# A fused DeltaNet and SwiGLU kernel: the small products ordered by tile shape and mixed across units, and 32x32 blocks moved through DRAM

## The chip, the cores and the metric

The kernel runs on one core of one Trainium2 chip. The metric is device time in microseconds (us): the median of the runs. The core has a matrix engine (PE, or TensorE; its weight loads are a queue of their own, PEld), a vector engine (DVE), a scalar engine (ACT), a general engine (POOL) and a queue that issues DMAs (SP). Each engine works through its instructions in the order of the program, and waits where an operand isn't there.

## What is computed

Two parts, both in float32. The first is a delta-rule attention over 4 batches (B), 8 heads (H), 768 tokens (S), head width 48 (D). With the keys normed to length 1, each head runs over its tokens:

```python
y[:, :, t] = np.einsum('bhd,bhde->bhe', q[:, :, t], state)
v_old = np.einsum('bhde,bhd->bhe', state, kt)
state = state + bt[:, :, :, None] * np.einsum('bhd,bhe->bhde', kt, vt - v_old)
```

The second takes y as 3072 rows of 384 and computes a gated feed-forward net (FFN): RMS norm with gain, g = xn @ w_gate, val = xn @ w_val, out = (silu(g) * val) @ w_out, with d_ff = 1536. The weights arrive as 64-bit floats, and the kernel turns their bits into float32 itself.

## The kernel before, in words

The tokens are cut into 6 chunks (NCH) of 128. A unit is one batch in one chunk, with its 8 heads; there are 24 units (n = 4c + b). In a chunk the recurrence becomes a triangular system, which is solved by halves of 64 (lo and hi) and quarters of 32. Each unit goes through four generators, and a chunk through a fifth:

- `prepare` norms the keys, transposes q and k on PE (p_t) into `kqt`, and makes all products of keys with keys and with queries (p_g, L293: four matrices of 64x64 inputs, 192 columns each). One DVE instruction per p_g (L300) multiplies by a mask and writes `gp`.
- `invert`, once a chunk for all 32 heads, inverts the 32x32 unit triangles on DVE: four 32x32 block transposes bring `gp` into `gblk` (L316), 31 steps of two instructions (L325, L334) build the inverse `ttb`, and transposes and copies (L336 to L351) put it into `tt`.
- `merge` joins the 32-quarters into 64-halves: p_v (L366) takes 32 rows and 64 columns of the array, p_w (L379) 32 by 32, and p_x (L388) 64 by 64 for the coupling of the halves, with copies on ACT between them.
- `recur` subtracts what the state already knows (p_k, L413), solves for u (p_z: L425 for both halves by 64x64, then L433 for the lower half, which needs the upper half's u), updates the state (p_s, L443), and makes the output p_y from the state (L453) and from u (L463 for the upper half, 64 rows by 64 columns; L466 for the lower half, 128 rows by 64 columns; the two alternate head by head). Then come the RMS norm and a transpose into `xt`.
- `ffn`, two a chunk, takes 256 tokens: for each of 12 slices of d_ff six matrix products into p_gv (L532), silu on ACT, a product h_f on DVE (L543), and two products into p_o (L519).

A float32 product is two PE instructions, so the trace counts twice as many as the program.

The order of the work is made by a plan. Each generator has a start time and yields after each piece with a step in plan units, and `run_plan` always continues the generator with the smallest time. One FFN piece (six instructions of p_gv, or four of p_o) is one unit; a chunk has 72. So small pieces fall between FFN pieces on PE. In a chunk, all merges stand at 46 to 48, and the recurs start at 50.1 and every 2.7 later. `weights` converts the 36 weight tiles on DVE and ACT, from plan time -69 on, one every 2.1 units. All small products share four PSUM buffers (tag "delta"). SP issues all DMAs, in order.

Of the kernel before, what the change touches and what calls it, by code (L numbers as in the profile page):

```python
# [10 lines left out]
FP32 = mybir.dt.float32  # L11
# [7 lines left out]
C = 128  # L19
HC = 64  # L20
DP = 64
W = 32
K1, K0, Q0, Q1 = 0, 2, 3, 4
# [4 lines left out]
def kernel(  # L28
# [11 lines left out]
):  # L40

# [23 lines left out]
    work = ctx.enter_context(tc.tile_pool(name="work", bufs=2))  # L65
    psum = ctx.enter_context(
# [8 lines left out]
    mask = const.tile([128, 3 * HC], FP32, name="mask")  # L75
# [16 lines left out]
    kqt = [const.tile([128, NP, 5, HC], FP32, name=f"kqt{b}") for b in range(B)]  # L92
    gp_all = const.tile([128, BH, 3 * HC], FP32, name="gp")
# [3 lines left out]
    back = const.tile([128, W, BH], FP32, name="back")  # L97

    vraw = {}

# [79 lines left out]
    raws = []  # L180
# [8 lines left out]
    def weights(dt):  # L189
        with tc.tile_pool(name="bits", bufs=2) as bits:  # L190
            fetch(bits)
            fetch(bits)
            yield dt
            for i, (dst, src) in enumerate(todo):
# [13 lines left out]
                )  # L208
                nc.scalar.activation(
# [16 lines left out]
                nc.vector.scalar_tensor_tensor(  # L226
                    out=exp,
                    in0=high,
                    scalar=0x80000000,
                    in1=exp,  # L230
                    op0=ALU.bitwise_and,
                    op1=ALU.bitwise_or,
                )
                nc.vector.scalar_tensor_tensor(
                    out=dst, in0=low, scalar=2.0**-52, in1=dst, op0=ALU.mult, op1=ALU.add
                )
                nc.vector.tensor_tensor(out=dst, in0=dst, in1=exp_f, op=ALU.mult)
                yield dt


    def prepare(n):
# [29 lines left out]
        nc.scalar.copy(kqt[b][:, :, Q0 : Q1 + 1], p_t)  # L271
# [10 lines left out]
        nc.scalar.copy(kqt[b][:, :, K0], p_t[:, :, 0])  # L282
        nc.scalar.copy(kqt[b][:, :, K1], p_t[:, :, 1])
        yield 2

        for g in range(NP // 2):
            p_gs = [ps_delta([128, 2, 3 * HC], "p_g") for par in range(2)]
            for jj in range(2):
                pair = kqt[b][:, 2 * g + jj]
                for par, i in ((0, 0), (1, 1), (0, 1), (1, 0)):  # L290
                    lo = slice(DP * par, DP * (par + 1))
                    rhs = pair[lo, K1 : K1 + 5 : 2] if i else pair[lo, K0 : K0 + 3]
                    nc.tensor.matmul(  # L293
                        p_gs[par][HC * i : HC * (i + 1), jj].rearrange("p (a t) -> p a t", a=3),
                        pair[lo, K1 if i else K0],
                        rhs,
                        skip_group_check=True,
                    )
            for par in range(2):
# [6 lines left out]
            yield 1  # L306

# [3 lines left out]
    def invert(c, dt):  # L311
        nc.gpsimd.memset(ttb, 0.0)
        nc.gpsimd.memset(ttb.rearrange("p j i -> p (j i)")[:, 0 : W * W : W + 1], 1.0)
        for a in range(NBLK):
            p, o = slice(W * a, W * (a + 1)), W * (a % 2)
            nc.vector.transpose(  # L316
                out=gblk[p], in_=gp_all[p, :, o : o + W].rearrange("p x j -> p j x")
            )
        yield dt
        for i in range(W - 1):  # L320
            n = W - 1 - i
            shape = [128, n, i + 1]
# [10 lines left out]
            to = ttb[:, i + 1 :, 0 : i + 1]  # L333
            nc.vector.tensor_tensor(out=to, in0=to, in1=tmp, op=ALU.add)  # L334
            yield dt
        nc.vector.transpose(out=back, in_=ttb)  # L336

        def place(a, copy):
            p, o = slice(W * a, W * (a + 1)), W * (a % 2)
            copy(tt_all[p, :, o : o + W].rearrange("p x j -> p j x"), back[p])  # L340

        place(1, nc.scalar.copy)
        place(3, nc.scalar.copy)

        nc.vector.tensor_tensor(
            out=gblk,
            in0=ttb.rearrange("p m s -> p s m"),
            in1=nbeta[:, c, None, :].to_broadcast([128, W, W]),
            op=ALU.mult,
        )  # L350
        nc.vector.transpose(out=ttb, in_=gblk)  # L351
        yield dt
        place(0, nc.vector.tensor_copy)
        place(2, nc.vector.tensor_copy)
# [266 lines left out]
```

## Time and profile before

| what | value |
|---|---|
| median of 3 runs | 1129.95 us (1114.73 to 1134.86) |
| the profiled execution | 1130.28 us, span 1128.5 us |
| PE busy | 1006.1 us (89% of the span) |
| DVE busy | 485.6 us (43%) |
| ACT busy | 275.8 us (24%) |
| chain that ended last | PE 70%, DVE 21%, ACT 4% |

In a row of a timeline stand the start (us from the span's start), the length (us), the engine, the line, the operation, the tile written and those read, the array tile used (rows*columns), the shape, and xcount, the number of instructions that are merged into the row. What is in brackets is the engine's idle time before it and what ended it. The lengths of PE rows overlap a little, since products are pipelined; start to start is the better reading.

### The profile page before, as it was taken

Reading aid. Unit: us, or ns where it says so; the run is one execution under the profiler, and the core shown is the slowest. Engines: PE = TensorE matmul, PEld = TensorE weight load, DVE = VectorE, ACT = ScalarE, POOL = GpSimd, SP = SyncE. Lnnn points to the kernel's source line nnn. Section 1 sums busy time; section 2 is a strip of 40 time slices with the busy share of each in tenths; the row PEclk is TensorE's granted clock in tenths of the full one; section 3 lists DMA queues with packets and bytes.
Section 4 is the critical chain, followed back from the end, with each engine's and each line's share of the span. In section 5 each row is a group of like instructions: output and inputs, shape, how many; then the busy total and the mean of one; then the engine's idle time right before and its main releaser. Section 6 shows DMA issues by size and latency. Waiting matters only on the chain.

```text
span 1128.5 us, 18814 instructions
## 1 busy us (share of the span) xinstructions
PE 1006.1 (89%) x8142; PEld 773.5 (69%) x8142; DVE 485.6 (43%) x1116; ACT 275.8 (24%) x590; POOL 83.3 (7%) x97
## 2 busy tenths in 40 slices
PE   5202997989999989999989999989999989999998
PEld 3102975767877767777767877767777767777776
DVE  5998347483222394222395122295132394211110
ACT  3766446113112112112112212112212113111011
POOL 6000003000021000022000022000021000000000
PEclk9555559998979996998998989998999998978999
DMA  6533222000111000011100011100011000000000
GB/s 146 138 95 96 72 72 76 8 15 2 29 22 35 15 15 1 18 34 29 22 15 1 16 36 29 22 15 1 16 37 28 1 15 1 2 1 15 1 15 15
DMA packets 84882, 34.43 MB, mean 31 GB/s; under 512 B 77088, under 2 KB 80160, under 8 KB 84800
## 3 DMA queue, kind: packets, MB, share of 16 engines
q1 hardware_dynamic: 84800, 33.24, 11.8%
q8 instruction: 64, 1.05, 0.4%
q14 instruction: 18, 0.15, 0.0%
HBM read 28.51 MB, written 4.72 MB: 29 GB/s over the span
## 4 chain that ended last, share of the span: by engine, by line
PE 70%; DVE 21%; ACT 4%; issue 1%; POOL 1%; POOLq 0%; ACTq 0%
PE p_gv L532 27%; PE p_o L519 12%; DVE tmp L325 6%; DVE ttb L334 5%; PE p_y L466 5%; PE p_y L463 5%; DVE gblk L316 4%; PE p_v L366 4%; PE p_g L293 3%; PE p_x L388 2%; PE p_z L425 2%; PE p_z L433 2%; PE p_w L379 2%; ACT tt L340 2%; PE p_k L413 1%; DVE h_f L543 1%
## 5 line engine op out<-in xcount | busy, mean ns | idle before, releaser
L519 PE MATMUL p_o<-wo_sb,h_f 128*128 128x384 f32 x576 | 220.3, 507 | 23.1 <-DVE h_f L543 23.1
L532 PE MATMUL p_gv<-xt,wv_sb 128*128 128x256 f32 x864 | 232.0, 408 | 0.0
L532 PE MATMUL p_gv<-xt,wg_sb 128*128 128x256 f32 x864 | 231.4, 406 | 0.0
L532 PEld LDWEIGHTS p_gv<-xt,wg_sb 128*128 128x128 f32 x864 | 169.2, 201 | 44.4 <-issue 2.6
L532 PEld LDWEIGHTS p_gv<-xt,wv_sb 128*128 128x128 f32 x864 | 171.6, 205 | 28.0 <-issue 3.1
L543 DVE TENSOR_TENSOR h_f<-sil,p_gv 128x256 f32<-128x256 f32 x144 | 59.9, 416 | 254.9 <-ACT sil L541 254.4
L519 PEld LDWEIGHTS p_o<-wo_sb,h_f 128*128 128x128 f32 x576 | 108.7, 196 | 78.5 <-DVE h_f L543 29.4
L541 ACT ACTIVATE sil<-p_gv 128x256 f32<-128x256 f32 x144 | 55.2, 384 | 413.0 <-PE p_gv L532 395.0
L366 PE MATMUL p_v<-tt,gp 32*64 32x32 f32 x768 | 44.6, 285 | 74.7 <-ACT tt L340 74.7
L366 PEld LDWEIGHTS p_v<-tt,gp 32*64 32x64 f32 x768 | 43.1, 207 | 79.6 <-ACT tt L340 79.6
L325 DVE SCALAR_TENSOR_TENSOR tmp<-gblk,nbeta,ttb 128x31 f32<-128x31 f32 (+15 forms) x186 | 74.3, 399 | 4.6
L300 DVE TENSOR_TENSOR gp<-p_g,mask 128x384 f32<-128x384 f32 x96 | 49.2, 551 | 52.5 <-PE p_g L293 52.5
L466 PE MATMUL p_y<-u,gp 128*64 128x48 f32 x384 | 66.3, 259 | 0.0
L334 DVE TENSOR_TENSOR ttb<-ttb,tmp 128x31 f32<-128x31 f32 (+15 forms) x186 | 63.5, 341 | 5.0
L463 PE MATMUL p_y<-u,gp 64*64 64x48 f32 x384 | 65.2, 254 | 0.0
L293 PE MATMUL p_g<-kqt 64*64 64x192 f32 x768 | 51.6, 365 | 12.8 <-DVE gp L300 6.5
L485 ACT ACTIVATE sq<-p_y 128x384 f32<-128x384 f32 x24 | 11.8, 491 | 185.7 <-PE p_y L466 185.7
L293 PEld LDWEIGHTS p_g<-kqt 64*64 64x64 f32 x768 | 28.9, 144 | 35.0 <-issue 13.9
L466 PEld LDWEIGHTS p_y<-u,gp 128*64 128x64 f32 x384 | 40.8, 150 | 11.9
L463 PEld LDWEIGHTS p_y<-u,gp 64*64 64x64 f32 x384 | 40.0, 146 | 13.0
L316 DVE STREAM_TRANSPOSE gblk<-gp 32x1024 f32<-32x1024 f32 x24 | 46.2, 1926 | 0.5
L252 POOL TENSOR_TENSOR knrm<-ksum,half 128x8 f32<-128x8 f32 x24 | 39.4, 1645 | 58.4 <-DVE ksum L250 58.3
(88 smaller groups left out, 893.2 us busy)
## 6 DMA issues: line engine op xcount, KB each, us to landing
kpad<-in_k_dram SPq DMA_DIRECT2D x24, 192.0 KB, 2.7
qpad<-in_q_dram SPq DMA_DIRECT2D x24, 192.0 KB, 2.6
v_raw<-in_v_dram SPq DMA_DIRECT2D x24, 192.0 KB, 3.1
raw<-in_moe_w_gate_dram SPq DMA_DIRECT2D x12, 384.0 KB, 3.2
raw<-in_moe_w_val_dram SPq DMA_DIRECT2D x12, 384.0 KB, 3.2
raw<-in_moe_w_out_dram SPq DMA_DIRECT2D x12, 384.0 KB, 3.0
out_dram<-o_sb SPq DMA_DIRECT2D x24, 192.0 KB, 1.9
beta_sb<-in_beta_dram SPq DMA_DIRECT2D x1, 96.0 KB, 3.3
```

The lines of the kernel that those rows point to most:

```text
L293: nc.tensor.matmul(p_gs[par][HC * i : HC * (i + 1), jj].rearrange("p (a t) -> p a t", a=3), pair[lo, K1 if i else K0], rhs, skip_group_che ...
L300: nc.vector.tensor_tensor(out=gp[b][:, 4 * g + par : 4 * g + 4 : 2], in0=p_gs[par], in1=mask[:, None, :].to_broadcast([128, 2, 3 * HC]), o ...
L316: nc.vector.transpose(out=gblk[p], in_=gp_all[p, :, o : o + W].rearrange("p x j -> p j x"))
L325: nc.vector.scalar_tensor_tensor(out=tmp, in0=gblk[:, i, i + 1 :, None].to_broadcast(shape), scalar=nbeta[:, c, i : i + 1], in1=ttb[:, i : ...
L334: nc.vector.tensor_tensor(out=to, in0=to, in1=tmp, op=ALU.add)
L366: nc.tensor.matmul(p_v[HC * (a // 2) : HC * (a // 2 + 1), h], gp[b][w, h, 0:HC], tt[b][w, h, W:HC], skip_group_check=True,)
L463: nc.tensor.matmul(p_y[lo, h], sc[lo, h, HC : 2 * HC], u[lo, h], start=first, stop=True, skip_group_check=True)
L466: nc.tensor.matmul(p_y[hi, h], sc[:, h, 2 * HC : 3 * HC], u[:, h], start=first, stop=True, skip_group_check=True)
L519: nc.tensor.matmul(p_o[i], h_f[:, i * C : (i + 1) * C], wo_sb[:, f], start=(f == 0), stop=(f == FT - 1),)
L532: nc.tensor.matmul(p_gv[:, i], w_sb[:, t, f * 128 : (f + 1) * 128], xt[:, t], start=(t == 0), stop=(t == KT - 1),)
L541: nc.scalar.activation(out=sil, in_=p_gv[:, 0], func=ACTF.Silu)
L543: nc.vector.tensor_tensor(out=h_f, in0=sil, in1=p_gv[:, 1], op=ALU.mult)
```

## The change

The change has five parts.

1. P U. `gp` gets four blocks a head instead of three, with a block of zeros below the upper half's scores, so that both halves of p_y from u use all 128 rows (128x64 tiles, L435).
2. Order. `merge` and `recur` of four units become one generator a chunk, `recur(c, dt)`. It goes through the units s = -3 to 5 in three pieces each: `inner` (64x64 tiles: p_z of unit s, its lower half for unit s-1, p_x of unit s+1), `outer` (128x64 tiles: p_k of unit s+1, p_y and p_s of unit s-1), `corner` (32x32 tiles: p_v of unit s+3 and p_w of unit s+2). In each piece the products of the units alternate head by head.
3. Blocks. The diagonal 32x32 blocks go from `gp` to DRAM (`gd`) and from there into `gblk`; the inverse goes to DRAM (`td`, and `nd` for its scaled form) and from there into `tt` and `ne`. The DVE transposes and the copies are gone.
4. Eviction of p_g. Instead of one DVE instruction there are two ACT copies and three smaller DVE instructions, and the mask is 64 wide.
5. Plan. All FFN pieces stand 16 units later against the rest; weights follow a list of steps, and the last three DVE instructions of a weight tile are issued one tile later.

```diff
-K1, K0, Q0, Q1 = 0, 2, 3, 4
+Q0, K0, Q1, K1 = range(4)
...
+            nc.gpsimd.memset(gp_all[HC:C, :, 0:HC], 0.0)
...
             for par in range(2):
+                to = gp[b][:, 4 * g + par : 4 * g + 4 : 2].rearrange("p h (a t) -> p h a t", a=4)
+                p_g = p_gs[par]
+                nc.scalar.copy(to[:, :, K0], p_g[:, :, K0])
+                nc.scalar.copy(to[hi, :, K1], p_g[hi, :, K1])
                 nc.vector.tensor_tensor(
-                    out=gp[b][:, 4 * g + par : 4 * g + 4 : 2],
-                    in0=p_gs[par],
-                    in1=mask[:, None, :].to_broadcast([128, 2, 3 * HC]),
-                    op=ALU.mult,
+                    out=to[lo, :, Q0], in0=p_g[lo, :, Q0], in1=over[lo], op=ALU.mult
+                )
+                nc.vector.tensor_copy(out=to[lo, :, Q1], in_=p_g[lo, :, Q1])
+                nc.vector.tensor_tensor(
+                    out=to[hi, :, Q1], in0=p_g[hi, :, Q1], in1=over[hi], op=ALU.mult
                 )
             yield 1
+        if b == 0:
+            gds[c] = dram.tile([128, W, W], FP32, name="gd")
+        for a in range(NBLK):
+            o = diagonal(a)
+            nc.sync.dma_start(
+                out=gds[c][a * BH + b * H : a * BH + (b + 1) * H].rearrange("h r j -> r h j"),
+                in_=gp[b][W * a : W * (a + 1), :, o : o + W],
+            )
+        if b == B - 1:
+            nc.sync.dma_start(out=gblk, in_=gds.pop(c))
...
-        for a in range(NBLK):
-            p, o = slice(W * a, W * (a + 1)), W * (a % 2)
-            nc.vector.transpose(
-                out=gblk[p], in_=gp_all[p, :, o : o + W].rearrange("p x j -> p j x")
-            )
...
+        nc.sync.dma_start(out=td, in_=ttb)
...
+        nc.sync.dma_start(out=nd, in_=gblk)
+        for b in range(B):
+            for a in (1, 3, 0, 2):
+                o = W * (a % 2)
+                nc.sync.dma_start(
+                    out=tt[b][W * a : W * (a + 1), :, o : o + W],
+                    in_=td[a * BH + b * H : a * BH + (b + 1) * H].rearrange("h r j -> r h j"),
+                )
+            for a in (0, 2):
+                nc.sync.dma_start(
+                    out=ne[W * a : W * (a + 1), b * H : (b + 1) * H],
+                    in_=nd[a * BH + b * H : a * BH + (b + 1) * H].rearrange("h r j -> r h j"),
+                )
...
+            for h in range(H):
+                for p, place in ((lo, Q0), (hi, Q1)):
+                    nc.tensor.matmul(
+                        p_y[p, h],
+                        gp[b_y][:, h, HC * place : HC * (place + 1)],
+                        u[:, h],
...
+        for s in range(-3, B + 2):
+            inner(s, s - 1, s + 1)
+            yield dt
+            outer(s + 1, s - 1)
+            yield dt
+            corner(s + 3, s + 2)
+            if s - 2 in units:
+                transpose_y(B * c + s - 2, ys.pop(s - 2))
+            yield dt
...
-    at(-69, weights(2.1))
     for c in range(NCH):
-        t0 = CYC * (c - 1)
+        t0 = CYC * c
         for b in range(B):
-            n = B * c + b
-            at(t0 - 1 + 5 * b, prepare(n))
-            at(t0 + 46 + 0.6 * b, merge(n, 2.7))
-            at(t0 + 50.1 + 2.7 * b, recur(n, 3))
-        at(t0 + 25.3, invert(c, 0.55))
+            at(t0 - 60 + 5 * b, prepare(B * c + b))
+        at(t0 - 32.7, invert(c, 0.55))
+        at(t0 - 9, recur(c, 1.2))
         for g in range(B // 2):
-            at(CYC * c + CYC // 2 * g, ffn(B // 2 * c + g))
+            at(t0 + 16 + CYC // 2 * g, ffn(B // 2 * c + g))
+
+    at(-59, weights([2.4] * 10 + [0.7] * 3 + [16] + [1.0] * 3 + [2.0] * 19))
```

The first place is PE at the output of a unit in the second chunk, before. A row names the line, the operation, the tile written, the tiles read and the shape written.

```order
L532 MATMUL p_gv<-xt,wg_sb 128x256 x3
L443 MATMUL p_s<-u,kpad_82 64x48 x8
L453 MATMUL p_y<-state_85,kqt_90 64x96 x8
L463 MATMUL p_y<-u,gp 64x48
L466 MATMUL p_y<-u,gp 64x48
```

The last two rows come eight times in turn, once a head, before the next FFN piece. With the change the same place on PE reads:

```order
L587 MATMUL p_gv<-xt,wg_sb 128x256 x3
L470 MATMUL p_k<-state_89,kqt_94 64x96 x8
L470 MATMUL p_y<-state_87,kqt_92 64x96 x8
L435 MATMUL p_y<-u,gp 64x48 x16
L448 MATMUL p_s<-u,kpad_84 64x48 x8
```

All of it uses 128x64 tiles now, the sixteen products from u stand in one row, and the p_k of a unit two further on has moved in front of them.

The second place is PE a little earlier in the same chunk, where units are merged and solved. Before, it reads:

```order
L413 MATMUL p_k<-state_87,kqt_92 64x96 x8
L425 MATMUL p_z<-v_raw,tt 64x48 x16
L532 MATMUL p_gv<-xt,wg_sb 128x256 x3
L433 MATMUL p_z<-u,x_2131 64x48 x8
L532 MATMUL p_gv<-xt,wv_sb 128x256 x3
```

With the change PE has there the end of a corner, an FFN piece and the begin of an inner:

```order
L401 MATMUL p_v<-tt,gp 32x32
L408 MATMUL p_w<-vs,ne 32x32
L574 MATMUL p_o<-wo_sb,h_f 128x384 x2
L488 MATMUL p_z<-v_raw,tt 64x48 x2
L497 MATMUL p_z<-u,x_2239 64x48
L506 MATMUL p_x<-tt,gp 64x64
```

The eight L433 of a unit, which stood alone, now stand singly between two products of the next unit's p_z and one p_x of the unit after, each on a 64x64 tile of its own; these three rows come eight times. In the first chunk the L497 still stand eight in a row.

The third place is SP in the second chunk, from the last blocks of `gp` to the first blocks of the inverse. Before, SP has there only loads of q and the output:

```order
L110 DMA qpad_83<-in_q_dram 128x8x48
L110 DMA qpad_84<-in_q_dram 128x8x48
L555 DMA out_dram<-o_sb 128x384 x2
L118 DMA v_raw<-in_v_dram 128x8x48 x3
L103 DMA kpad_82<-in_k_dram 128x8x48
```

With the change:

```order
L119 DMA qpad_86<-in_q_dram 128x8x48
L326 DMA gd<-gp 32x8x32 x8
L331 DMA gblk<-gd 128x1024
L610 DMA out_dram<-o_sb 128x384 x2
L358 DMA td<-ttb 128x1024
L366 DMA nd<-gblk 128x1024
L370 DMA tt<-td 32x8x32 x4
L375 DMA ne<-nd 32x8x32 x2
```

The last two rows come four times, so a chunk has 43 more DMAs on SP: 16 of gd, one of gblk, td, nd, 16 of tt and 8 of ne.

## Rows read from the trace of the kernel before

**Rows 1.** Stretches: length, busy PE, PEld, DVE, ACT, POOL, PE clock, DMA share, GB/s
```profile
105.00:165.00 60.00, 59.27 (x706) 52.13 (x707) 24.53 (x58) 24.77 (x55) 2.85 (x5) 0.50 0.29 74
346.00:516.00 170.00, 163.29 (x1380) 124.73 (x1378) 69.85 (x155) 32.56 (x74) 13.22 (x14) 0.92 0.09 20
1040.00:1126.00 86.00, 85.05 (x349) 65.89 (x347) 9.27 (x22) 10.36 (x26) 0.00 (x0) 1.00 0.02 6
```
**Rows 2.** Timeline of PE, one unit's state and output in the third chunk
```profile
480.25 0.67 PE L443 MATMUL p_s<-u,kpad 128*64 128x48 f32 x16
480.75 0.85 PE L453 MATMUL p_y<-state,kqt 128*64 128x96 f32 x16
481.53 0.31 PE L463 MATMUL p_y<-u,gp 64*64 64x48 f32 x2
...
485.42 2.92 PE L532 MATMUL p_gv<-xt,wv_sb 128*128 128x256 f32 x6
```
**Rows 3.** Timeline of PE, the 64x64 products of the same chunk
```profile
460.02 2.08 PE L388 MATMUL p_x<-tt,gp 64*64 64x64 f32 x32
462.03 0.88 PE L413 MATMUL p_k<-state,kqt 128*64 128x96 f32 x16
...
469.74 1.14 PE L425 MATMUL p_z<-v_raw,tt 64*64 64x48 f32 x32
470.81 1.56 PE L532 MATMUL p_gv<-xt,wg_sb 128*128 128x256 f32 x6
472.30 1.13 PE L433 MATMUL p_z<-u,x 64*64 64x48 f32 x16
473.36 1.56 PE L532 MATMUL p_gv<-xt,wv_sb 128*128 128x256 f32 x6
...
490.64 0.25 PE L433 MATMUL p_z<-u,x 64*64 64x48 f32 x1
490.68 0.23 PE L425 MATMUL p_z<-v_raw,tt 64*64 64x48 f32 x2
...
490.85 0.92 PE L433 MATMUL p_z<-u,x 64*64 64x48 f32 x13
```
**Rows 4.** Timeline of PE, the 32-row products of the same chunk
```profile
435.06 7.03 PE L366 MATMUL p_v<-tt,gp 32*64 32x32 f32 x124 [0.35 <-ACT tt L340]
...
448.79 2.03 PE L379 MATMUL p_w<-vs,ttb 32*32 32x32 f32 x64
450.75 2.93 PE L532 MATMUL p_gv<-xt,wg_sb 128*128 128x256 f32 x6
```
**Rows 5.** Timeline of PE, two waits of the same chunk
```profile
415.26 1.56 PE L519 MATMUL p_o<-wo_sb,h_f 128*128 128x384 f32 x4 [2.47 <-DVE h_f L543]
433.08 0.41 PE L366 MATMUL p_v<-tt,gp 32*64 32x32 f32 x4 [1.60 <-ACT tt L340]
```
**Rows 6.** Timeline of DVE and PE in the first chunk
```profile
100.04 0.18 DVE L334 TENSOR_TENSOR ttb<-ttb,tmp 128x31 f32<-128x31 f32 x1
105.73 0.53 PE L366 MATMUL p_v<-tt,gp 32*64 32x32 f32 x6 [0.89 <-ACT tt L340]
129.74 1.09 PE L443 MATMUL p_s<-u,kpad 128*64 128x48 f32 x16
130.76 0.45 PE L463 MATMUL p_y<-u,gp 64*64 64x48 f32 x2
131.13 0.45 PE L466 MATMUL p_y<-u,gp 128*64 128x48 f32 x2
...
164.99 1.49 PE L532 MATMUL p_gv<-xt,wg_sb 128*128 128x256 f32 x3
```
**Rows 7.** DMA issues: tensor, queue, count, KB each, median us to landing
```profile
kpad<-in_k_dram SPq DMA_DIRECT2D x24, 192.0 KB, 2.7
raw<-in_moe_w_gate_dram SPq DMA_DIRECT2D x12, 384.0 KB, 3.2
nbeta<-in_beta_dram SPq DMA_DIRECT2D x4, 24.0 KB, 2.1
```

More of the change, by code (lines that the diff above doesn't have):

```diff
@@ L96, with diagonal @@
     ttb = const.tile([128, W, W], FP32, name="ttb")
-    back = const.tile([128, W, BH], FP32, name="back")
+    ne = const.tile([128, BH, W], FP32, name="ne")
     vraw = {}
+    lo, hi = slice(0, HC), slice(HC, C)
+    def diagonal(a):
+        return HC * (K1 if a >= 2 else K0) + W * (a % 2)
     def load_k(n):
@@ L225, in weights, with rest @@
                 )
[L226 to L238, printed above, removed]
+                if last is not None:
+                    rest(*last)
+                last = (dst, low, high, exp)
+                yield dts[i]
+            rest(*last)
+    def rest(dst, low, high, exp):
+        nc.vector.scalar_tensor_tensor(
+            out=exp,
+            in0=high,
+            scalar=0x80000000,
+            in1=exp,
+            op0=ALU.bitwise_and,
+            op1=ALU.bitwise_or,
+        )
+        nc.vector.scalar_tensor_tensor(
+            out=dst, in0=low, scalar=2.0**-52, in1=dst, op0=ALU.mult, op1=ALU.add
+        )
+        nc.vector.tensor_tensor(out=dst, in0=dst, in1=exp.bitcast(FP32), op=ALU.mult)
     def prepare(n):
@@ L332, in invert @@
             )
-            to = ttb[:, i + 1 :, 0 : i + 1]
+            to = ttb[:, 0 : i + 1, i + 1 :]
             nc.vector.tensor_tensor(out=to, in0=to, in1=tmp, op=ALU.add)
             yield dt
[L336 to L343, printed above, removed]
+        td = dram.tile([128, W, W], FP32, name="td")
@@ L382, in merge @@
-        for a in (0, 2):
-            w = slice(W * a, W * (a + 1))
-            nc.scalar.copy(tt[b][w, :, W:HC], p_w[w])
-        yield dt
-        p_x = ps_delta([128, H, HC], "p_x")
-        for h in range(H):
-            nc.tensor.matmul(
-                p_x[0:HC, h],
-                gp[b][HC:C, h, HC : 2 * HC],
-                tt[b][HC:C, h],
-                skip_group_check=True,
-            )
-        x2 = work.tile([HC, H, HC], FP32, name="x2", bufs=B)
-        nc.scalar.mul(x2, p_x[0:HC], -1.0)
@@ L483, in recur, with norm @@
+            if b_x in units:
+                x2s[b_x] = work.tile([HC, H, HC], FP32, name="x2", bufs=3)
+                nc.scalar.mul(x2s[b_x], p_x[lo], -1.0)
+        ys = {}
+        for s in range(-3, B + 2):
[7 more added lines that the diff above has]
+            yield dt
+    def norm(p_y):
         sq = work.tile([128, DM], FP32, name="sq", bufs=1)
```

262 lines of the change are left out of this document (139 added, 123 removed).

## Prediction

> **What bounds the kernel now.** The chain of work that ended last is read first: 70% of it is PE, so the next view is the busy time by stretch [rows 1]. The reader is to see three regimes there. From 105 to 165 us PE is busy all the time at a granted clock of 0.50, with the merges and recurs of the first chunk; no FFN product has run yet. In a whole chunk (346 to 516) PE is busy 163.3 of 170 us, at a mean clock of 0.92. At the end only FFN is left, and PE runs at 1.00. DVE is busy 70 of 170 us and ACT 33, so from 165 us on PE's own time is what the kernel lasts, and before it DVE's.
>
> The timelines of PE then say what a chunk's 170 us are. In the last stretch 349 instructions are FFN alone; at 16 for a slice of d_ff that is 21.8 slices in 86 us, 3.94 us each, so the 24 slices of a chunk take about 95 us [rows 1]. The other 75 us are small products, waits of PE, and FFN groups at half clock.
>
> **P U.** The 32 instructions of p_y from u last from 481.53 to 485.42, 3.89 us or 122 ns each. The 16 of p_s last 0.50 us, 31 ns each [rows 2]. Both stream 48 columns; the difference is that the first alternate between 64*64 and 128*64 tiles and the second stay on one shape. On one shape I price them at p_s's 31 ns: 4 units x 32 x 31 ns = 4.0 us instead of 15.6, a gain of 11.6 us a chunk. The upper bound of their price is p_y from the state, 16 in 0.78 us or 49 ns [rows 2], although that has 96 columns: gain 9.2. A lower price than 31 ns has no row. The rows of zeros add no instruction.
>
> **64x64 products (inner).** Alone on one tile, p_x takes 2.01 us for 32 (63 ns) and the lower half of p_z 1.06 us for 16 (66 ns); p_z on two tiles takes 1.07 us for 32 (33 ns). So a tile gives one product every 63 to 66 ns, and two tiles work beside each other. Where the scheduler happened to mix three tiles, the nine instructions that start from 490.64 up to 490.85 take 0.21 us, 23 ns each [rows 3]. Before, a chunk has 64 x 63 + 128 x 33 + 64 x 66 ns = 12.5 us of them. After, the first p_x and the last lower half stay alone (16 x 63 + 16 x 66 ns = 2.1 us), two pieces mix three tiles (96 x 23 ns = 2.2), and two mix four (128 instructions). Four tiles have no row with so few columns: 66/4 = 16.5 ns would be the full gain, 23 ns none beyond three. I take 18, nearer to the full gain because two and three tiles both scaled almost in full: 2.3 us. Sum 6.6, gain 5.9 us (5.3 to 6.1; at the two-tile 33 ns for all that is mixed 3.0).
>
> **32x32 products (corner).** p_v takes 7.03 us for 124, 57 ns each, p_w 1.96 us for 64, 31 ns [rows 4]: 128 of each are 11.2 us. After, both load 32 columns, and in three of five pieces they alternate on four tiles. The lone p_v and the lone p_w cost 64 x 31 ns = 2.0 us, the rest 192 x 18 ns = 3.5 us; gain 5.7 us (3.3 if all stay at 31 ns, 6.0 at 16).
>
> **Clock and waits.** After p_w a p_gv group takes 2.93 us, after P U 2.92, where at full clock, with the same change of tile, it is 1.56 [rows 2 to 4]. A mean clock of 0.92 over 170 us is 27 us at half clock. With P U cut to a quarter and p_v no longer one block of 7 us, but pieces of about a microsecond between FFN groups, I take 4 us a chunk as won; the bounds are 0 and 0.5 x 27 = 13.6. PE waits 170 - 163.3 = 6.7 us a chunk [rows 1], among others 2.47 for an h_f that stands behind the inversion on DVE, and 1.60 for the copies into `tt` [rows 5]. The four block transposes and the copies go, and the blocks of the inverse now have 8.5 plan units, at least 11 us, to come. In return the first step of the inversion waits on DVE for gblk, with the h_f products of FFN queued behind it, and PE waits for those. The round trip is some 2.1 us for small blocks (nbeta) and 3.2 to 3.7 for 512 KB (raw brings 384 KB in 3.2) plus the issues [rows 7], against five plan units or about 7 us: late by a microsecond or two. I take 2 us won (bounds: 4 lost, 5 won). The added ACT copies (32 a chunk) and DVE pieces cost nothing, because ACT is busy 33 and DVE 70 us of 170 [rows 1]; if they sit on a wait they are part of the rival of the waits.
>
> A chunk then gains 11.6 + 5.9 + 5.7 + 4 + 2 = 29.2 us, and the five chunks whose small work lies beside FFN gain 146 us.
>
> **The start.** From 105.73 to 164.99 PE works on the first chunk at half clock [rows 6]. There p_s is 64 ns an instruction (16 from 129.74 to 130.76) and P U 0.37 us a pair, 185 ns. 128 x (185 - 64) ns = 15.5 us go. p_v at p_w's price saves 3.3. The lower halves of p_z still stand eight in a row here, so nothing is taken for them. The last unit's output moves behind the first FFN products, which only moves it. Against this: the inverse ends at 100.2 and p_v starts in full at 105.73, 5.5 us later, by way of DVE and ACT; through DRAM it takes about 3.3 us to write td, 3.0 to issue four DMAs and 2.1 to land, 8.4 us, so 3 us more. With shorter pieces the chain product, copy, product of one unit shows, and DVE and ACT still have weights in their queues: 4 us. DVE loses four transposes ahead of the inversion, but waits for the round trip of gblk, partly under weights: nothing. That is 15.5 + 3.3 - 3 - 4 = 12 us; the weights that are ready earlier give some more against the waits that follow 165 us, so I take 15 (bounds: 5 lost, 22 won).
>
> **Sum.** The profiled execution took 1130.3 us (span 1128.5), within 0.4 us of the median of the runs. 1130.3 - 146 - 15 = 969 us. With all low bounds together (9.2 + 3.0 + 3.3 + 0 - 4 = 11.5 a chunk, start 5 lost) it would be 1078, with all high ones (11.6 + 6.1 + 6.0 + 13.6 + 5 = 42.3 a chunk, start 22) 897.
>
> **The rivals.**
>
> Starts have a floor. If the 23 ns of the three-tile row are the least that PE needs from one start to the next, a fourth tile brings nothing: 320 instructions a chunk at 23 instead of 18 ns are 1.6 us, times 5 is 8 us less: 977 us. For it: no stretch of the trace goes below 23 ns. Against it: from one tile to three the pace went in proportion, from 66 to 23 ns, so up to there it was the tile that set it [rows 3]. The Trainium skill (TensorE: Matmul & The Clock Gate, "Wait — 56ns, not 53.3ns?") has such a floor at about 25 ns, however few the columns; the nine starts in 0.21 us lie just under it, and by it the sum would be 981 us.
>
> Two tiles are all. If what paces small products is not the tile but the loads or the issue, inner and corner stay at 31 to 33 ns where they are mixed. For it: p_w, p_s and p_z all stand near 31 ns, whatever their size. Against it: the nine starts at 23 ns. Inner gives 3.0 and corner 3.3 instead of 5.9 and 5.7: 5.3 x 5 = 27 us less, 996 us.
>
> The clock comes back. If the small pieces are short enough between FFN groups that the clock stays at 2.4 GHz, the chunk gains 10 us instead of 4: 939 us. For it: groups after a p_z of 1 us run at full length 1.56 [rows 3]. Against it: the pieces of outer, some 3 us, are as long as P U was.
>
> Waits replace products. A chunk's recur is now a chain of 27 pieces with a copy by ACT or DVE between them, in four shared PSUM buffers, of which p_z holds one through two pieces and outer wants three more. If each piece meets a wait of half a microsecond (the wait for tt was 1.60 [rows 5]), 13.5 us a chunk come back: 969 + 68 = 1037 us. Against it: between two pieces stand 1.2 FFN groups, 1.5 us, and a copy takes about 0.4 to 0.6.
>
> The blocks through DRAM decide, and the kernel is slower. The 24 DMAs that bring back the inverse follow each other on SP. At nbeta's pace (four issues in 3 us) they take 18 us. The last unit's corner comes 19 plan units after the inversion ends, 19 x 141/72 = 37 us. If each DMA had to land before the next is issued, the point from which this decides is 2.75 us for one: the last blocks then come 66 us after the inversion, 29 us late, and the gain of a chunk is gone. At kpad's 2.7 us and half a microsecond of issue they are 40 us late, and the start loses 77 us less the 25 that lie under its products: 969 + 5 x 40 + 52 = 1221 us. For it: these DMAs have pieces of 128 bytes, and the trace shows no write of such pieces to DRAM. Against it: 1024 pieces of 192 bytes land in 2.7 us [rows 7], nbeta's pieces of 128 bytes in 2.1. The Trainium skill (DMA: Bandwidth & Descriptors, Specifications) says that pieces under 512 bytes are done by read-modify-write, and that line rate needs 512; no run here shows what that costs for a write.
>
> **How the numbers follow.** Forecast 0.42 (its own range 950 to 990), floor 0.14, two tiles 0.12, clock 0.10, waits 0.16, DRAM decides 0.06. The range 925 to 1040 takes in all but the last and the tails of the others. A difference of 2% is about what a measurement of this kernel can tell (the three runs lie 1.8% apart). Faster by over 2%, below 1107: all but the last, 0.94. Within 2%: 0.02, a half-way form of the last. Slower: 0.04, the rest of it.
>
> **What would show it.** Right: P U at 31 ns with one shape in the timeline, 1.0 us a unit; mixed inner and corner rows at 16 to 20 ns; a chunk of about 141 us between the starts of two inversions; the first p_gv at about 150 us; the clock in a chunk near 0.95. Wrong: waits of PE in front of p_w, p_z or p_y that sum to over 10 us a chunk; p_v waiting for a DMA into `tt`; DVE waiting for gblk for more than 3 us; P U above 49 ns, which would say that the change of shape was not what made it slow.

## The result and the profile after

The changed kernel takes 914.8 us (median of 4 runs, 910.4 to 917.0) against 1127.8 for the kernel before beside it (1114.7 to 1134.9): a ratio of 0.814, 95% interval 0.806 to 0.822. The forecast of 969 us was 54 us too high, and the result lies below its range. The profiled execution took 912.8 us, with a span of 911.0.

Busy time by stretch of the changed kernel: the end of the start, a whole chunk, and FFN alone; columns as in [rows 1].

```profile
110.00:146.00 36.00, 30.37 (x669) 27.40 (x664) 16.55 (x41) 21.78 (x50) 1.98 (x3) 0.99 0.49 111
280.00:410.00 130.00, 129.26 (x1363) 98.39 (x1358) 61.26 (x176) 37.10 (x102) 11.90 (x14) 1.00 0.20 46
800.00:900.00 100.00, 100.00 (x555) 78.49 (x554) 13.96 (x33) 13.89 (x36) 1.62 (x3) 1.00 0.02 9
```

Where [rows 1] show PE busy 163.3 of 170 us at a clock of 0.92, a chunk now has it busy 129.3 of 130 at 1.00. The timeline of DVE has the last step of the first inversion and the first step of the next two:

```profile
101.97 0.21 DVE L354 TENSOR_TENSOR ttb<-ttb,tmp 128x31 f32<-128x31 f32 x1
...
201.05 0.25 DVE L345 SCALAR_TENSOR_TENSOR tmp<-gblk,nbeta,ttb 128x31 f32<-128x31 f32 x1
...
333.00 0.24 DVE L345 SCALAR_TENSOR_TENSOR tmp<-gblk,nbeta,ttb 128x31 f32<-128x31 f32 x1
```

The period of a chunk is 132 us; before, the same step starts at 403.34 and 575.43, 172 us apart. So a chunk gains 40 us where 29.2 were forecast. Between the two profiled executions the miss is 56 us: 4 at the start, and 52 behind the first FFN product, some 10.5 in each of five chunks.

The timeline of PE in the changed kernel, at the start and in the third chunk, answers to [rows 2 to 4, 6]:

```profile
109.68 1.14 PE L401 MATMUL p_v<-tt,gp 32*32 32x32 f32 x32 [62.36 <-DMA tt<-td]
...
130.38 1.06 PE L448 MATMUL p_s<-u,kpad 128*64 128x48 f32 x16
136.15 0.64 PE L448 MATMUL p_s<-u,kpad 128*64 128x48 f32 x16
...
145.80 2.93 PE L587 MATMUL p_gv<-xt,wg_sb 128*128 128x256 f32 x6 [1.53 <-DVE xt L561]
...
365.47 0.69 PE L401 MATMUL p_v<-tt,gp 32*32 32x32 f32 x32
366.10 1.56 PE L587 MATMUL p_gv<-xt,wg_sb 128*128 128x256 f32 x6
...
378.51 0.21 PE L401 MATMUL p_v<-tt,gp 32*32 32x32 f32 x1
378.51 0.21 PE L408 MATMUL p_w<-vs,ne 32*32 32x32 f32 x1
...
379.19 1.56 PE L587 MATMUL p_gv<-xt,wv_sb 128*128 128x256 f32 x6
380.68 0.26 PE L488 MATMUL p_z<-v_raw,tt 64*64 64x48 f32 x2
380.70 0.27 PE L506 MATMUL p_x<-tt,gp 64*64 64x64 f32 x1
...
381.77 1.56 PE L574 MATMUL p_o<-wo_sb,h_f 128*128 128x384 f32 x4
...
389.02 0.26 PE L488 MATMUL p_z<-v_raw,tt 64*64 64x48 f32 x2
389.04 0.25 PE L497 MATMUL p_z<-u,x 64*64 64x48 f32 x1
389.04 0.27 PE L506 MATMUL p_x<-tt,gp 64*64 64x64 f32 x1
...
390.12 1.56 PE L587 MATMUL p_gv<-xt,wg_sb 128*128 128x256 f32 x6
...
391.61 0.88 PE L470 MATMUL p_k<-state,kqt 128*64 128x96 f32 x16
...
392.98 1.09 PE L435 MATMUL p_y<-u,gp 128*64 128x48 f32 x32
393.90 0.64 PE L448 MATMUL p_s<-u,kpad 128*64 128x48 f32 x16
394.46 1.56 PE L587 MATMUL p_gv<-xt,wv_sb 128*128 128x256 f32 x6
395.95 0.69 PE L408 MATMUL p_w<-vs,ne 32*32 32x32 f32 x32
396.58 1.56 PE L574 MATMUL p_o<-wo_sb,h_f 128*128 128x384 f32 x4
```

Read start to start: P U, 392.98 to 393.90, is 29 ns an instruction instead of 122. A corner of p_v and p_w, 64 instructions from 378.51 to 379.19, is 10.6 ns an instruction; p_v and p_w alone are 20 ns (0.63 us for 32). An inner of three tiles, 380.68 to 381.77, is 48 at 22.7 ns, one of four, 389.02 to 390.12, 64 at 17.2. A whole outer, 391.61 to 394.46, is 2.85 us. Every FFN group behind these pieces takes 1.56 us, where [rows 2, 4] had 2.92 and 2.93 behind P U and p_w. At the start the inversion ends at 102, hardly later than the 100 of [rows 6]; the first FFN product comes at 145.80 instead of 164.99. A second profiled execution of the changed kernel (e10) has it at 151.26: there p_s still takes 1.06 us at 138.85 and 146.66, where here it is back at 0.64 from 136.15 on. So a difference of up to 5.5 us at the start can be chance.

The waits of PE: us in total, times, longest. First the kernel before, in the two rows that [rows 5] give one case each of:

```profile
PE p_v L366 <- ACT tt L340: 74.7, 12, 64.6
PE p_o L519 <- DVE h_f L543: 23.1, 13, 2.5
```

Then the changed kernel:

```profile
PE p_v L401 <- DMA tt<-td: 62.6, 2, 62.4
PE p_o L574 <- DVE h_f L598: 3.7, 5, 0.7
```

The longest wait of each p_v row is that of the start. Without it PE waited 10.1 us for `tt` and 23.1 for h_f before; 0.2 and 3.7 are left. DVE shows no wait for `gblk` at all. The DMAs that replace the transposes (count, KB each, median us to landing):

```profile
gd<-gp SPq DMA_DIRECT2D x96, 32.0 KB, 1.6
gblk<-gd SPq DMA_DIRECT2D x6, 512.0 KB, 3.2
td<-ttb SPq DMA_DIRECT2D x6, 512.0 KB, 2.6
tt<-td SPq DMA_DIRECT2D x96, 32.0 KB, 2.1
```

### The profile page after: what moved, and what is told of

Read it like the earlier page. It is cut to its first block, busy times and chain, and to the rows that moved or that the text cites. A ratio compares the mean times of both kernels' runs of the same rounds, so it can differ in the third digit from the quotient of the medians.

```text
span 911.0 us, 19658 instructions
## 1 busy us (share of the span) xinstructions
PE 810.2 (89%) x8142; PEld 618.2 (68%) x8142; DVE 442.0 (49%) x1259; ACT 310.5 (34%) x770; POOL 85.8 (9%) x98
## 4 chain that ended last, share of the span: by engine, by line
PE 77%; DVE 15%; ACT 3%; issue 1%; DMA 1%; POOL 0%; DVEq 0%; ACTq 0%; POOLq 0%
PE p_gv L587 38%; PE p_o L574 18%; DVE tmp L345 4%; PE p_g L302 4%; DVE ttb L354 4%; PE p_y L435 2%; PE p_z L488 2%; PE p_k L470 2%; PE p_y L470 2%; PE p_x L506 2%; PE p_v L401 1%; PE p_t L277 1%; DVE exp L238 1%; PE p_w L408 1%; PE p_s L448 1%
## 5 line engine op out<-in xcount | busy, mean ns | idle before, releaser
L587 PE MATMUL p_gv<-xt,wg_sb 128*128 128x256 f32 x864 | 215.4, 386 | 1.5 <-DVE xt L561 1.5
L587 PE MATMUL p_gv<-xt,wv_sb 128*128 128x256 f32 x864 | 216.1, 387 | 0.0
L587 PEld LDWEIGHTS p_gv<-xt,wv_sb 128*128 128x128 f32 x864 | 162.2, 192 | 24.7 <-issue 2.8
L401 PE MATMUL p_v<-tt,gp 32*32 32x32 f32 x768 | 19.7, 201 | 62.6 <-DMA tt<-td 62.6
L401 PEld LDWEIGHTS p_v<-tt,gp 32*32 32x32 f32 x768 | 16.6, 113 | 72.2 <-ACT exp L225 62.9
L314 DVE TENSOR_TENSOR gp<-p_g,mask 64x128 f32<-64x128 f32 x96 | 26.9, 280 | 51.2 <-ACT gp L313 49.7
L549 POOL TENSOR_TENSOR rs<-ms,mhalf 128x1 f32<-128x1 f32 x24 | 13.5, 562 | 326.6 <-DVE ms L547 326.6
L312 ACT COPY gp<-p_g 128x128 f32<-128x128 f32 x96 | 25.4, 265 | 45.9 <-PE p_g L302 44.3
L488 PEld LDWEIGHTS p_z<-v_raw,tt 64*64 64x64 f32 x768 | 26.4, 142 | 8.8 <-issue 6.9
L416 ACT COPY vs<-p_v 32x256 f32<-32x256 f32 x48 | 17.4, 363 | 39.7 <-PE p_w L408 30.3
L506 PE MATMUL p_x<-tt,gp 64*64 64x64 f32 x384 | 29.9, 233 | 0.5 <-ACT tt L418 0.5
```

The source lines that it names most:

```text
L401: nc.tensor.matmul(p_v[wa, h], gp[b_v][wb, h, o : o + W], tt[b_v][wb, h, W:HC], skip_group_check=True,)
L488: nc.tensor.matmul(p_zs[b_z][p, h], tt[b_z][p, h], r[p, h], start=(h == 0), stop=(p is lo), skip_group_check=True,)
L506: nc.tensor.matmul(p_x[lo, h], gp[b_x][hi, h, HC * K0 : HC * (K0 + 1)], tt[b_x][hi, h], skip_group_check=True,)
L587: nc.tensor.matmul(p_gv[:, i], w_sb[:, t, f * 128 : (f + 1) * 128], xt[:, t], start=(t == 0), stop=(t == KT - 1),)
```

## The experiments

The table splits PE's time, start to start, from the first p_gv to the end, for every kernel whose parts are compared (in us; from each kernel's trace; idle time is that of over 0.15 us, which the timeline has in brackets). "Half clock" is a part of FFN: what its groups took beyond 0.248 us for an instruction of p_gv and 0.36 of p_o, counted where a row is over a quarter longer than that.

| kernel | median | first p_gv | FFN | half clock | P U | inner | corner | idle |
|---|---|---|---|---|---|---|---|---|
| before | 1127.8 | 165.0 | 625.2 | 37.0 | 80.5 | 58.4 | 55.8 | 37.9 |
| e1b: P U alone | 1030.3 | 148.9 | 610.4 | 24.7 | 20.3 | 58.4 | 59.2 | 29.9 |
| e6: narrow p_v alone | 1096.4 | 160.7 | 619.9 | 31.9 | 79.9 | 58.4 | 33.7 | 36.4 |
| e7: both | 1001.0 | 143.7 | 605.9 | 19.6 | 20.3 | 58.4 | 39.0 | 30.3 |
| changed | 914.8 | 145.8 | 587.5 | 3.6 | 20.0 | 32.4 | 16.5 | 7.3 |
| e10: changed, once more | 917.2 | 151.3 | 586.2 | 2.8 | 19.7 | 32.3 | 16.5 | 7.3 |
| e2: P U as before | 1016.0 | 163.5 | 601.8 | 17.5 | 79.0 | 32.8 | 17.2 | 7.6 |
| e3: not mixed | 946.3 | 152.3 | 587.1 | 3.3 | 19.7 | 54.4 | 21.9 | 7.5 |
| e4: blocks by DVE | 972.2 | 149.9 | 598.9 | 7.4 | 19.7 | 32.4 | 29.0 | 38.5 |
| e12: e4, p_w's weights dense | 971.9 | 152.9 | 602.3 | 10.7 | 19.7 | 32.4 | 21.3 | 39.1 |
| e5: wide p_v | 1055.6 | 153.6 | 611.4 | 25.9 | 19.7 | 39.7 | 119.7 | 7.5 |

The theory is that the miss sits in the term "Clock and waits": that changes of tile shape lower the clock of what follows, and that the block transposes on DVE made PE wait. The rival is that both come from the mixing of units in short pieces.

### P U on two shapes again (e2)

```diff
-    gp[b_y][:, h, HC * place : HC * (place + 1)],
-    u[:, h],
+    gp[b_y][lo if p is lo else slice(0, C), h, HC * place : HC * (place + 1)],
+    u[lo if p is lo else slice(0, C), h],
```

> The changed kernel, with one edit: the upper half of P U goes back to 64 rows, so that 64x64 and 128x64 tiles alternate again. If P U is worth its own instructions only, the time is 915 + 60 + 13 = about 988 us and the clock stays near 0.99. If the alternation is what lowers the clock, it falls to about 0.93 and the time is 1010 us or more.

Measured: 1016.0 us (1011.4 to 1019.3), ratio to before 0.897 (0.890 to 0.905). One unit's P U and what follows it on PE (the first row merges both shapes and shows that of its first instruction):

```profile
429.55 4.40 PE L435 MATMUL p_y<-u,gp 64*64 64x48 f32 x31
433.62 0.34 PE L448 MATMUL p_s<-u,kpad 128*64 128x48 f32 x1
433.75 0.31 PE L435 MATMUL p_y<-u,gp 128*64 128x48 f32 x1
433.75 1.15 PE L448 MATMUL p_s<-u,kpad 128*64 128x48 f32 x15
434.84 2.93 PE L587 MATMUL p_gv<-xt,wv_sb 128*128 128x256 f32 x6
```

The part is worth 101 us: 59 in its own instructions, 18 at the start (12 against e10), 14 in FFN, nearly all at half clock (17.5 instead of 3.6), 6 in p_s, which stands behind it (15.5 instead of 9.6 us), and the rest spread. So the alternation does lower the clock of what follows: nothing else was changed, and PE is idle for 7.6 us here as for 7.3 there. It explains 14 of the 38 us that FFN lost, no more.

### P U on one shape in the kernel before (e1b)

The upper half reads a tile `gq` with zeros below it, which four small DVE instructions a unit fill.

```diff
-    p_y[lo, h], sc[lo, h, HC : 2 * HC], u[lo, h], start=first, stop=True, skip_group_check=True
+    p_y[lo, h], gq[b][:, h], u[:, h], start=first, stop=True, skip_group_check=True
```

> The kernel before with one part of the change alone: the upper half of P U reads a block with zeros below it, so that all of P U uses 128x64 tiles (four small DVE instructions a unit are added for that block; one mask buffer less). Order, blocks through DRAM, 32x64 tiles of p_v stay as before. In the trace of before 15.6 us of half-clock FFN groups stand right behind P U, 7.1 behind p_v, 4.2 behind p_w, 4.1 behind p_xt, 3.9 behind waits. Theory A (P U costs its own instructions only, what makes the clock fall is something else): 60 us beside FFN and 15 at the start go, 1134 - 75 = about 1058, and half-clock groups still stand behind P U. Theory B (the alternation of tile shapes is what lets the clock fall): 15 us more, about 1043, and no half-clock group behind P U. Rival (the freed time turns into waits of PE, since DVE and ACT still move the blocks): above 1070, idle of PE well above the 38 us of before.

Measured: 1030.3 us (1027.6 to 1032.8), ratio 0.912 (0.909 to 0.914); 99 us of the change come from this part alone. It went 13 us below theory B, mostly because idle time fell by 8 as well, and because the kernel before took 1129.8 us beside it, where 1134 was taken. The start gained 16 us, as expected. Half-clock groups right behind p_y fell from 15.5 to at most 0.5 us; those behind p_v and p_w did not go but grew (from 11.4 to 21.6).

### p_v on 32x64 or 32x32 tiles (e5, e6, e7)

In e5 the changed kernel gets wide weights for p_v again:

```diff
-    p_v[wa, h],
-    gp[b_v][wb, h, o : o + W],
+    p_v[W * a : W * a + HC, h],
+    gp[b_v][wb, h, o : o + HC],
```

> The changed kernel with p_v back on 32x64 tiles (64 weight columns, of which 32 are used); pieces, mixing, P U and DRAM blocks as changed. Theory A (p_v costs its own instructions only): a lone p_v at 57 instead of 20 ns is 128 x 37 ns = 4.7 us a chunk where nothing runs beside it, 24 in all, less where p_w runs beside it: 925 to 940, FFN as in the changed kernel (585 us). Theory B (p_v on wide tiles is also what let the clock fall behind it): 5 to 10 us more in the FFN groups behind the corner: 940 to 950. If p_v in short pieces costs neither, it stays within 5 us of 915.

Measured: 1055.6 us (1054.4 to 1058.4), ratio 0.935 (0.932 to 0.938). Both theories miss by over 100 us, and the timeline of PE in two corners, p_v alone and p_v with p_w, says why:

```profile
400.63 1.12 PE L401 MATMUL p_v<-tt,gp 32*64 32x32 f32 x32
401.69 1.56 PE L587 MATMUL p_gv<-xt,wg_sb 128*128 128x256 f32 x6
...
405.76 0.30 PE L401 MATMUL p_v<-tt,gp 32*64 32x32 f32 x2
405.99 0.24 PE L408 MATMUL p_w<-vs,ne 32*32 32x32 f32 x2
406.16 0.30 PE L401 MATMUL p_v<-tt,gp 32*64 32x32 f32 x2
...
409.83 0.42 PE L401 MATMUL p_v<-tt,gp 32*64 32x32 f32 x2
...
410.41 0.42 PE L401 MATMUL p_v<-tt,gp 32*64 32x32 f32 x2
...
413.35 2.93 PE L587 MATMUL p_gv<-xt,wg_sb 128*128 128x256 f32 x6
```

I had overlooked that p_v and p_w then alternate between two shapes. Four instructions with two changes take 0.40 us (405.76 to 406.16). Without changes they take at least 4 x 10.6 ns, and at most what the lone ones take, 2 x 33 (1.06 us for the 32 from 400.63) and 2 x 20: so a change costs 0.15 to 0.18 us. In [rows 2] the four instructions of a head take 0.49 us, of which 4 x 29 ns are their own: about 0.185 us a change, although there the rows change (64 and 128) and here the columns. And from 409.83 on, inside the alternation, the pace falls to 0.58 us for four, with an FFN group of 2.93 behind it. So the corner that is mixed on two shapes is slower, at 119.7 us, than before without mixing (55.8): mixing pays only after sorting by shape. The lone wide p_v at 33 ns also corrects the 57 of [rows 4], which the expectation used: in the kernel before, the granted clock is 0.50 from 434.5 to 442, all through that block of p_v, so the 57 were a price at half clock.

In e6 the kernel before gets the narrow p_v alone, with one more ACT instruction for each copy into `vs`:

```diff
-    p_v[HC * (a // 2) : HC * (a // 2 + 1), h],
-    gp[b][w, h, 0:HC],
+    p_v[W * (a - 1) : W * a, h],
+    gp[b][w, h, 0:W],
```

> The kernel before with p_v on 32x32 tiles alone (32 weight columns instead of 64; its copy to vs is made in two ACT instructions). Order, P U, blocks as before. Own instructions: 57 to 31 ns or less, 128 x 26 ns = 3.3 us a chunk, 17 to 20 us in all: about 1115. If the 7.1 + 4.2 us of half-clock groups behind p_v and p_w come from it as well: about 1104. Waits for tt stay as before (1.6 us a chunk), since DVE and ACT still make it; if p_v is bound by its wait for tt and not by its tiles, it stays above 1125.

Measured: 1096.4 us (1095.2 to 1097.7), ratio 0.970 (0.968 to 0.973): 33 us, more than expected. By the profiled executions 22 lie in the corner, 5 in FFN, 4 at the start. Part of the corner's 22 is clock, since the wide p_v ran at half clock. e7 has both parts.

> The kernel before with both of these parts: P U on one shape and p_v on 32x32 tiles. If the two add up, with their clock: about 1043 - 25 = 1018; own instructions only: about 1038. What is then left to the changed kernel (915) is the order with its mixing (e3 puts that at 31 us without the pieces) and the blocks through DRAM (e4 puts that at 57): 1018 - 31 - 57 = 930, so the parts should nearly close the sum.

Measured: 1001.0 us (996.5 to 1007.8), ratio 0.886 (0.882 to 0.891): 129 us, and 99 + 33 is 132, so the two add up. Half-clock groups are left behind p_w (8.2 us) and p_v (7.6), though both are on 32x32 tiles now. In the changed kernel, where they stand in pieces with FFN between, there are none. But two things differ there: in e7 PE still waits for `tt` ahead of p_v, and in the changed kernel it doesn't. e4 below has the pieces and the waits.

### Not mixed (e3)

In each piece the products of one unit go out together, then those of the next: a `for h in range(H):` ahead of each group, instead of one around all of them.

> The changed kernel, with one edit: in corner and inner the products of one unit are issued all together, and then those of the next, instead of alternating head by head; pieces, plan and tiles stay. If the tile sets the pace, inner goes back to some 12 us a chunk (from 6.4) and corner to 5 (from 3.3), together 36 us in five chunks: about 950 us at an unchanged clock. If the mixing is also what keeps the clock up, the clock falls below 0.97 and the time is 970 or more. If mixing is worth nothing (scheduling hides it), 915.

Measured: 946.3 us (943.5 to 946.8), ratio 0.836 (0.831 to 0.841). The mixing is worth 31 us: 22 in inner, 5 in corner, 6 at the start (1 against e10). FFN is the same, 587.1, and so are half clock, 3.3, and idle time, 7.5. So far as it is mixing head by head, the rival falls: that has no part in the clock or the waits. The short pieces stayed, and no run takes them away alone.

### Blocks by DVE and ACT (e4, e12)

```diff
+        for a in range(NBLK):
+            p, o = slice(W * a, W * (a + 1)), diagonal(a)
+            nc.vector.transpose(
+                out=gblk[p], in_=gp_all[p, :, o : o + W].rearrange("p x j -> p j x")
+            )
...
+        nc.vector.transpose(out=back, in_=ttb.rearrange("p r j -> p j r"))
...
+        nc.vector.transpose(out=ne, in_=gblk.rearrange("p r j -> p j r"))
```

The DMAs of `gd`, `gblk`, `td`, `nd`, `tt` and `ne` go, and four copies bring `back` into `tt`, as before.

> The changed kernel, with one edit: the 32x32 blocks go through DVE transposes and copies as before, and the DMAs through DRAM are left out; order, tiles and plan stay. If the waits of PE went because DVE was relieved of the blocks, they come back: 6 us a chunk, about 940 to 945 us. If they went because the new order and plan leave more room, the time is within 10 us of 915, and a start some 3 to 5 us earlier (no way through DRAM before the first p_v) may even make it a little faster.

Measured: 972.2 us (971.3 to 973.8), ratio 0.859 (0.854 to 0.864): the DMAs are worth 57 us, twice what was expected. The waits of PE in e4:

```profile
PE p_v L389 <- ACT tt L353: 82.5, 12, 67.6
PE p_o L562 <- DVE h_f L586: 21.0, 25, 2.6
```

Both waits are back, and idle time is 38.5 us instead of 7.3. What h_f stands behind on DVE, in the timeline of e4:

```profile
339.78 5.83 DVE L329 STREAM_TRANSPOSE gblk<-gp 32x1024 f32<-32x1024 f32 x3
346.10 1.93 DVE L329 STREAM_TRANSPOSE gblk<-gp 32x1024 f32<-32x1024 f32 x1
...
374.56 1.97 DVE L349 STREAM_TRANSPOSE back<-ttb 128x1024 f32<-128x1024 f32 x1
378.23 1.01 DVE L353 COPY tt<-back 32x1024 f32<-32x1024 f32 x1
```

The transposes into `gblk` are 1.93 us each, up to three of them in a row, 5.83 us, while an h_f takes 0.42. DVE being busy for 41% of a chunk told nothing of that. The longest wait for h_f in a chunk, 2.55 us at 363.11, comes only in the middle of the inversion's steps; that DVE is still behind from the transposes there is my reading, but the wait is 0.74 us in the changed kernel, with the same steps.

By the profiled executions (58.6 us apart) the difference is 31 us of idle time, 12 in the corner, 11 in FFN and 4 at the start. The clock has a part in it: 5.9 of e4's 7.4 us at half clock stand behind waits, as from 382.55, where PE has waited 0.95 and 1.72 us for `tt` and 0.59 for h_f, and the granted clock is 0.53 in the next 2.7 us. So waits of PE, too, come before a fall of the clock, and the half clock behind p_v and p_w went in two steps: 15.8 us in e7, these 5.9 in e4, none in the changed kernel. How much of the first step is the pieces and how much the rest of the order isn't shown.

The corner's 12 had a suspect of its own: in e4, as before, the numbers of `ne` or `ttb` that make a row of p_w's weights lie 128 bytes apart; the DMAs leave them in a run. e12 is e4 with them in a run.

```diff
-    ne = const.tile([128, W, BH], FP32, name="ne")
+    ne = const.tile([128, BH, W], FP32, name="ne")
...
-        nc.vector.transpose(out=ne, in_=gblk.rearrange("p r j -> p j r"))
+        nc.vector.transpose(out=ne.rearrange("p x j -> p j x"), in_=gblk.rearrange("p r j -> p j r"))
...
-    p_w[wa, h], ne[wa, :, b_w * H + h], vss[b_w][wa, h], skip_group_check=True
+    p_w[wa, h], ne[wa, b_w * H + h], vss[b_w][wa, h], skip_group_check=True
```

> The kernel of e4 (blocks by DVE and ACT, no DRAM), with one thing as in the changed kernel: the scaled inverse `ne` lies block by block, so that a row of p_w's weights is 32 numbers in a run; in e4, as in the kernel before, they lie 128 bytes apart. The weight loads of p_w take 144 to 145 ns in before and e4 and 111 in the changed kernel, and a lone p_w 32 against 20 ns. Theory A (spread weights make the corner slow): corner 28.9 falls to about 17 us, as in the changed kernel, and the time by 8 to 12 us, to 960 to 964; what remains against 915 is DVE and ACT (waits for h_f and tt). Theory B (it is the waits or the clock around it): corner stays at 25 us or more and the time within 4 us of 972.

Measured: 971.9 us (970.9 to 972.6), ratio 0.862 (0.860 to 0.864): no change. p_w's weight loads do fall, as the group of PEld in e4 and then in e12 shows (busy us, mean ns of one):

```profile
L396 PEld LDWEIGHTS p_w<-vs,ne 32*32 32x32 f32 x768 | 24.8, 144 | 5.8 <-issue 4.2 <-ACT vs L404 1.6
```

```profile
L396 PEld LDWEIGHTS p_w<-vs,ne 32*32 32x32 f32 x768 | 16.7, 113 | 5.8 <-issue 4.2 <-ACT vs L404 1.6
```

A lone p_w takes 19.5 ns instead of 32.0, at full clock both times. The corner falls from 29.0 to 21.3 us, so theory A holds for the instructions. But FFN rises by 3.4, all of it at half clock (10.7 instead of 7.4), behind the same waits for `tt`; the first p_gv comes 3.0 us later (152.9), which can be chance; and the end stays where it was: theory B for the time. Why the half clock lasts longer there stays open.

### A faster version (e8 to e11)

From 60 to 100 us in the changed kernel PE does nothing and DVE has no gap, with 13 weight tiles among the steps of the first inversion. In e8, 26 tiles take their bias from `late`, which is made of the inversion's result and so comes after it:

```diff
+        if c == 0:
+            nc.vector.scalar_tensor_tensor(
+                out=late, in0=ttb[:, 0, W - 4 : W], scalar=0.0, in1=lift, op0=ALU.mult, op1=ALU.add
+            )
...
-    at(-59, weights([2.4] * 10 + [0.7] * 3 + [16] + [1.0] * 3 + [2.0] * 19))
+    at(-59, weights([2.4] * 9 + [30] + [2.0] * 26))
```

> An attempt at a faster kernel: the changed kernel, in which 26 of the 36 weight tiles are converted only after the first inversion (their bias is made from its result, and the plan issues one every 2.0 units from then on); nothing else is changed. In the trace of the changed kernel DVE works without a gap from 60 to 100 us, the inversion with 13 weight tiles between its steps, five instructions and some 2 us a tile: 25 us. If the start is bound by that, the inversion ends near 77 instead of 102 us. The first chunk's products then run with weights between their copies, which costs 5 to 15 us of the 36 they take now, so the first p_gv comes near 130 instead of 146, and the time is 895 to 905. Rival: the weights only move behind the inversion into the chain of copies and in front of h_f, and the end stays within 1% of 915.

> As e8, but after the first 17 tiles one every 1.5 units instead of 2.0, so 23 instead of 21 tiles stand ahead of the first h_f and 31 instead of 25 ahead of the fourth slice's. If the first FFN slices wait for weights in e8, this one is faster by that wait; if the weights crowd the copies of the first chunk, it is slower by two tiles, 4 us. Expected within 5 us of e8.

In e9 the list of steps is [2.4] * 9 + [30] + [1.0] * 6 + [1.5] * 20.

Measured: e8 907.0 us (902.9 to 907.1), just above its range, e9 913.6 (910.8 to 918.1), 6.6 above e8. In e8 the inversion ends at 84, not 77, and the first p_gv comes at 132.8 instead of 145.8. Of these 13 us, 6 reach the end of the profiled executions (spans 905.3 and 911.0), because idle time after that is 11.5 instead of 7.3 us and FFN 589.8 instead of 587.5; against e10 it is 10 of 18. e9 has its first p_gv even earlier, at 128.5, and is not faster for it; from 146 to 276 us PE is busy 119.5 us there, 122.6 in e8 and 125.6 in the changed kernel.

> The changed kernel itself once more, for a comparison with the next one on the same chip. 915, ratio 0.814.

> The kernel of e8 once more (26 weight tiles converted after the first inversion). If the 8 us of e8 are real, 907 against 915 with intervals that do not overlap; if they were scatter, both within 3 us.

Measured: the changed kernel 917.2 us (916.7 to 917.9), ratio 0.813 (0.811 to 0.816); the kernel of e8 905.8 (902.2 to 907.3), ratio 0.802 (0.799 to 0.805). The gain of 11 us is real, 1.2%.

## Why the prediction was wrong

The parts close the sum. P U on one shape is 99 us (e1b), narrow p_v 33 (e6), the blocks by DMA 57 (e4), the mixing 31 (e3): 220, against 213 measured; the first two were measured in the kernel before, the others in the changed one. Pieces, plan and eviction of p_g were not taken away by themselves. The sum leaves no gain for them alone, but part of the half clock behind p_v and p_w went with them.

By the steps of the prediction, with the table's first and fifth row:

- **P U**, 58 us forecast for five chunks: 60.5. Right, with 29 ns for the 31 taken.
- **Inner**, 29.5: 26.0. Right, with 17.2 ns for four tiles (18 taken) and 22.7 for three (23).
- **Corner**, 28.5: 39.3. Too small by 11. The mixed pieces run at 10.6 ns, not 18, and p_v and p_w alone at 20, not 31. The 31 of [rows 4] was taken as the price of a 32x32 tile; it was that of weights 128 bytes apart. e6 shows a p_w at 32 ns where the FFN group behind it runs at full clock, so it was not the clock (e12: 19.5 ns with dense weights). The 57 of p_v was a price at half clock; at full clock a wide p_v takes 33 (e5). So part of what the corner gained is clock.
- **Clock and waits**, the step that failed: 6 us a chunk, 30 in all, were taken; FFN gave 37.7, of which 33.4 at half clock, and idle time 30.6, together 68. For the clock I took 4 us a chunk of bounds of 0 to 13.6; it was 7.5. The mechanism stood in the text (groups behind P U and p_w at half clock), but I argued that pieces of outer, as long as P U was, would keep the clock down. Length was not what counts: 2.85 us of outer on one shape leave the next group at 1.56 us, and P U on two shapes makes it 2.93 (e2). For the waits I took 2 us a chunk, by weighing a late `gblk` against them; it was 6, because `gblk` was not late, and because I never priced the transposes, 4 x 1.93 us a chunk ahead of h_f. Of the 37.9 us of idle time before, 32 were waits for h_f and `tt`; e4 brings them back, and only the blocks differ in it.
- **The start**, 15: 19.2, and 13.7 in e10. Right within what one execution can tell. p_v starts 7.5 us after the inversion, 8.4 forecast.

Three small slips in its sums change nothing: at 49 ns P U gains 9.3 us a chunk, not 9.2; at 16 ns the corner gains 6.2, not 6.0; and a floor of 25 ns gives 980 us, not 981.

The rivals: the floor of 23 ns falls with 10.6. So does the Trainium skill's floor of 25 ns (TensorE: Matmul & The Clock Gate, "Wait — 56ns, not 53.3ns?"): four tiles in turn start an instruction every 10.6 ns here, and the measurement decides. Two tiles fall with 17.2. The waits fall with 7.3 us of idle time in all, the DMAs with 0.2 us of waiting for `tt` after the start. "The clock comes back" (939 us, chance 0.10) came nearest: the clock of a chunk is 1.00, and FFN gave 7.5 us of its 10. But its reason, short pieces, isn't what the runs show: e2 has the same pieces on two shapes and loses the clock. Alone this rival would still have been 24 us too high; the waits and the corner make up the rest.

## What to carry to other kernels

Sort small products by tile shape first: here each change of shape costs 0.15 to 0.185 us, as much as 8 to 17 instructions on tiles that work beside each other (20 to 10.6 ns), and behind a run of 32 alternating instructions, some 4 us, the clock is at half. Then mix units on different tiles. Long instructions on an engine that is busy 41% of the time still count if a short one behind them is on the critical path: look for what stands in front of it, and move it to DMA where the round trip has time.

## What was not expected

- A change costs about as much between 64 and 128 rows (0.185 us) as between 64 and 32 columns (0.15 to 0.18). The Trainium skill (TensorEngine Tiling (Array Packing), Key Properties) says that a change of tiling mode, not of tile, drains the engine; the traces agree so far as turns of tiles of one shape cost nothing (10.6 ns an instruction), and give the price of a change. The drain itself is not seen in them.
- Writes to DRAM in pieces of 128 bytes landed in 1.6 us for 32 KB, faster than any read in [rows 7].
- The clock of the stretches does not always follow the lengths. In the changed kernel's start the row for 110 to 146 us has 0.99, yet p_s takes 1.06 us at 130.38 and 0.64 at 136.15. e8 and e11 are one program, both with 905 us of span, and the page's row of the clock, in 40 slices, reads so in e8 and then in e11:

```profile
PEclk9999999899999999999999999999999999999999
```

```profile
PEclk9965559999999999999999999999999999999999
```

In both, p_s takes 1.06 us near 110. Where the two differ, the length of a known instruction is the better witness.
